# GpSimd decodes from the start, the shared port passed on by explicit dependencies, and a new order

## The chip, the cores and the metric

The kernel runs on one core of one Trainium2 chip. The metric is the time of one launch on the device in microseconds. The engines are named as the profile names them: PE (TensorE; PEld is its loading of weights), DVE (VectorE), ACT (ScalarE), POOL (GpSimd) and SP (SyncE, which only issues DMAs here).

## What is computed

Three stages follow each other: a recurrent attention (mLSTM), then two feed-forward layers on its output. The attention is computed in chunks of 64 time steps; the recurrence below is what every chunk must reproduce.

```python
for t in range(S):                                   # B=4, H=8, S=768, D=40
    m_new = np.maximum(f_gate[:, :, t] + m, i_gate[:, :, t])
    f_stab = np.exp(f_gate[:, :, t] + m - m_new)
    i_stab = np.exp(i_gate[:, :, t] - m_new)
    C = f_stab * C + i_stab * outer(vt, kt)
    n = f_stab * n + i_stab * kt
    y[:, :, t] = sigmoid(o_gate[:, :, t]) * (C @ qt) / np.maximum(np.abs(n @ qt), 1.0)
x = y.transpose(0, 2, 1, 3).reshape(B * S, H * D)    # 3072 x 320
h = x @ w_in;  x = np.maximum(0.01 * h, h) @ w_out   # layer 0, d_ff = 2048
h = x @ w_in2; out = (h * np.cos(h)) @ w_out2        # layer 1
```

The weights come as float64 and are turned into float32 on the chip.

## The kernel before

**Tiles and stages.** The 3072 tokens are 24 chunks of 128 rows. Layer 0 takes them in blocks of 4, 2, 3, 3, 3, 3, 3, 3 chunks (`BLOCKS1`), layer 1 in eight blocks of 3. A block has 16 *slots*, one for each 128 columns of `d_ff`. In a slot PE multiplies into the hidden tile (`m_in`, L806, written "in(k)" here), ACT makes the rounded activation `gh` and the full one in place (L814, L815), DVE takes their difference `gl` (`m_lo`, L854, "gl(k)"), and PE multiplies both with the output weights (`m_out`, L874, "mo(k)"). Every matmul is split this way into a rounded and a rest part.

**Weights.** Each of the 16 pieces of a layer's weights is loaded as 704 KB of 64-bit words (`w_load`, L422) and decoded by six steps: on DVE a shift (`w_bits`, L432), on ACT the tail and the sign (`w_tail`, L436; `w_sign`, L440), on DVE or POOL an addition (`w_round`, L444), on DVE the mask (`w_mask`, L448). Then ACT rounds (`w_hi`, L217) and DVE or POOL subtracts (`w_lo`, L463). A slot's in(k) waits for piece k. Layer 0's pieces are decoded while block 0 runs.

**Attention.** For chunk c, DVE scans the gates (L597), scales k (`kt`, L616) and v (`vext`, L609), PE makes the scores (L636, L627), DVE weighs them (L643), PE makes output and state (`a_out`, L664, L672). DVE adds the state's part (`ys`, L710), ACT and DVE make the denominator (`norm`, L718; `rec`, L720, L721), DVE scales and gates (`scale`, L728; `gate`, L733, which writes the tile `x`); `decay` (L690) prepares the next state. Then the chunk is transposed into `xt`: PE turns it (`x_turn`, L516, into the only tile `tr`), ACT rounds (L217), PE subtracts (`x_neg`, L534, L535, chunks 0 to 3) and ACT copies the rest. in(0) of block 0 waits for `xt` of the chunks 0 to 3. `g_turn` (L355 to L372, twice: turn(0) and turn(1)) spreads gate values; turn(1) uses the tile `tr` too.

**Order.** The class `Schedule` places every step on an engine by planned durations, priorities (`MUST`, `OFF`, `OFF0` and the other numbers at the head) and rings of buffers. The instructions are then issued in the order of the planned starts, and each engine works its own list in that order. Steps that the plan marks "port" (those of DVE with SBUF operands alone, and all of POOL) never overlap in the plan, as DVE and POOL share a port of SBUF.

**Fillers and pace.** 95 matmuls `busy` (`g_busy`, L267) that compute nothing stand on PE between the steps of the start and of block 0. A filler, and a DMA planned between 10 and 100 us, waits for the last DVE instruction that the plan has ended by then (`PACE`, `PACED`). All fillers write one tile of the ring "h", which has two tiles; the hidden tiles of block 0 come from the same ring. In the built program the hidden tiles of the slots 0 to 9 have one PSUM bank and `busy` has the other, and the two banks alternate from slot 10 on.

The function that a filler runs:

```python
i = hpi.bitcast(BF16)[:, 0:1]
nc.tensor.matmul(gt["busy"], i.to_broadcast([P, P]), i.to_broadcast([P, 512]), start=True, stop=True)
```

Of the kernel before, what the change touches and what calls it, by code (L numbers as in the profile page):

```python
# [34 lines left out]
NG = 3  # L35
# [9 lines left out]
WC = 3 * P + DM  # L45
# [12 lines left out]
ATT_GAP = 6.901
ATT_STEP = 1.34
OUT_LAG = 4.678  # L60
SLOT0 = 1.284
DEC_LEAD = 51.726
BUSY = [0.9, 44.0, 0.22, 58.0]
BY_PE = (0, 1, 2, 3)
MUST = {0: -89.386, 1: -35.775, 2: 41.006, 3: -118.66, 4: 7.351, 5: 41.735, 6: 41.268, 7: -49.472, 8: 9.383, 9: 11.955, 10: -120.864, 11: -1.76, 12: -54.393, 13: 8.105, 14: 10.291, 15: 40.118, 16: -25.59, 17: 6.765, 18: 45.788, 19: 75.325, 20: 7.383, 21: -25.675, 22: 55.394, 23: 9.929, 24: 7.4, 25: 9.087, 26: 31.973, 27: 23.522, 28: 9.759, 29: -29.728, 30: 24.391, 31: 42.171, 32: 38.02, 33: 21.052, 34: 23.884, 35: 39.051}
SPREAD = 4
PACE = 0.05
PACED = [10.0, 100.0]
TURNS = {0: -9.044, 1: -47.963}
GATES_TOO = -4.817  # L70
W2 = {0: -16.972, 1: -35.024}
OFF = {
    "fb": 152.276, "kvo": -84.501, "qk": 75.164, "vext": 37.96, "scan": -34.694, "kt": 81.751, "s": 9.354, "weigh": 65.471, "out": 135.411,
    "sig": 169.166, "ym": -23.852, "ys": -10.938, "norm": -12.629, "scale": -18.623, "gate": 76.438, "state": 108.617, "decay": 20.307, "tr": 29.765,
    "x2": 16.41, "l_a": -90.166, "l_g": -57.684, "l_cos": 34.983, "l_mul": -67.795, "l_gh": 122.022,
    "l_gl": -11.238, "w_round": 136.001, "w_mask": 74.621, "w_hi": 58.111, "w_lo": -46.707, "w_load": -50.808,
}

OFF0 = {
    "decay": 136.328, "fb": -55.476, "gate": 90.467, "kt": 88.848, "kvo": 55.846, "norm": 95.847, "out": 125.427, "qk": 40.375, "s": 87.542, "scale": -4.774, "scan": 70.824, "sig": 93.266, "state": -25.01, "tr": -2.926, "vext": 205.41, "weigh": 110.435, "ym": -19.56, "ys": 54.077,  # L80
}
# [5 lines left out]
class Schedule:  # L87
# [13 lines left out]
    def run(self):  # L101
# [3 lines left out]
        while todo:  # L105
# [68 lines left out]
            if not drop:  # L174
                order.append((start, len(order), eng, fn, args, end, pace))
        return sorted(order, key=lambda o: o[:2])
# [3 lines left out]
def mlstm_moe(ctx, tc, qk, kvo, gates, w1, w2, out):  # L180
# [42 lines left out]
    def dve(n, fast=False):  # L223
        return ("DVE", 0.065 + n * (0.00053 if fast else 0.00105), "port")
# [240 lines left out]
    def plan_decode(l, i, p, after=0.0):  # L465
        k = (l, i)
        wide = dma(2 * WC if double[l] else WC, pace=True)
        if not double[l]:
            sch.add(("wload", k), p - 6, SP, w_load, l, i, take=[("wf", k, 1)], after=after, **wide)
            return ("wload", k)  # L470
        sch.add(("wload", k), p - OFF["w_load"], SP, w_load, l, i, take=[("raw64", k, 1)], after=after,
                **wide)
        sch.add(("bits", k), p, ("DVE", 0.435, "port"), w_bits, l, i, deps=[("wload", k)], take=[("wf", k, 1)])
        sch.add(("tail", k), p, act(WC), w_tail, l, i, deps=[("wload", k)])
        sch.add(("sign", k), p + 0.1, act(WC), w_sign, l, i, deps=[("wload", k)], take=[("sg", k, 1)])
        sch.add(("round", k), p + OFF["w_round"], [dve(WC)] + pool(WC, l), w_round, l, i, deps=[("bits", k), ("tail", k), ("sign", k)],
                free=[("raw64", k)])
        sch.add(("mask", k), p + OFF["w_mask"], dve(WC), w_mask, l, i, deps=[("round", k), ("sign", k)], free=[("sg", k)])
        return ("mask", k)

    def plan_split(l, i, p, dep):
        k = (l, i)
        sch.add(("whi", k), p, act(WC), w_hi, l, i, deps=[dep], take=[("w", k, 1)])
        sch.add(("w", k), p + OFF["w_lo"], [dve(WC)] + pool(WC, l), w_lo, l, i, deps=[("whi", k)], free=[("wf", k)])

# [57 lines left out]
    def plan_x(l, n, c, j, p, dep, src, ring, m):  # L543
# [193 lines left out]
    def plan_attention(n, c, j, m):  # L737
# [32 lines left out]
        sch.add(("out", c), e - off["out"], ("PE", 0.65 + (0.29 if not last else 0)), a_out, c,  # L770
                deps=[("weigh", c), ("vext", c)] + kt,
# [126 lines left out]
    def plan_layer(l, n, c0, m):  # L898
        N = m * P
        blocks = (BLOCKS1, BLOCKS2)[l]  # L900
        for i in range(NF):
# [63 lines left out]
    c = 0  # L965
# [73 lines left out]
```

## Time and profile before

| | us |
|---|---|
| median of 3 runs | 817.56 (815.19 to 817.56) |
| the profiled execution | 817.87 |
| its span | 816.1 |
| PE busy | 803.5 |
| DVE busy | 611.3 |
| ACT busy | 443.0 |
| POOL busy | 27.1 |

The span is what the instructions cover; 1.77 us of the execution lie around it. A row of a timeline gives the start, the duration, the engine, the line, the operation and its tiles, how many instructions were merged, and in brackets the engine's idle time before it with what ended that. Back-to-back instructions of DVE overlap a little in such rows, so the distance from start to start is what one of them costs. [...]

### The profile page before, as it was taken

The numbers are of one execution on the slowest core, as the hardware profiler recorded it, in microseconds if no ns is written. First come the engines' busy times: TensorE is split into PE (matmuls) and PEld (weight loads), VectorE is DVE, ScalarE is ACT, GpSimd is POOL, SyncE is SP. The second block draws the span as 40 slices with busy tenths as digits, with TensorE's granted clock in tenths as the row PEclk, the third lists the DMA queues.
The fourth block names the chain that finished last, engine by engine and source line by source line (L and its number), as shares of the span: only waits on it lengthen the run. The fifth ranks groups of instructions, "written<-read, shape, count | busy, mean of one in ns | idle before, by whom it ended". The sixth has DMA issues, their size and how long they took to land.

```text
span 816.1 us, 19170 instructions
## 1 busy us (share of the span) xinstructions
PE 803.5 (98%) x7803; PEld 767.3 (94%) x7815; DVE 611.3 (75%) x1287; ACT 443.0 (54%) x976; POOL 27.1 (3%) x29
## 2 busy tenths in 40 slices
PE   9899999999999999999999999999999999999998
PEld 5668899998999999999999999999999999999998
DVE  7979987747647478473738798889798988888886
ACT  3578844435534345344344665656565656565664
POOL 1000010000302000100000000000000000000000
PEclk9999999999999999999999999999999999999999
DMA  6655564516615254343324300000000000010000
GB/s 187 196 185 204 168 180 155 183 43 168 196 60 151 90 169 156 101 138 118 105 77 146 111 9 29 21 17 25 25 26 25 25 22 29 10 41 9 13 13 25
DMA packets 29944, 74.49 MB, mean 91 GB/s; under 512 B 4384, under 2 KB 13728, under 8 KB 29856
## 3 DMA queue, kind: packets, MB, share of 16 engines
q1 hardware_dynamic: 29856, 73.27, 28.9%
q8 instruction: 61, 1.00, 0.5%
q14 instruction: 27, 0.22, 0.1%
HBM read 59.54 MB, written 13.71 MB: 90 GB/s over the span
## 4 chain that ended last, share of the span: by engine, by line
PE 93%; DVE 5%; issue 1%; ACT 1%; DVEq 0%; ACTq 0%
PE acc L874 40%; PE ph L806 36%; PE pair L806 6%; PE busy L267 2%; PE tr L516 2%; PE pair L627 2%; PE pair L664 2%; PE pair L636 1%; PE pair L672 1%; DVE gl L854 1%; DVE wf L444 1%; DVE wf L448 1%; DVE w L463 1%; DVE wf L432 0%; DVE fb L643 0%
## 5 line engine op out<-in xcount | busy, mean ns | idle before, releaser
L874 PE MATMUL acc<-w,gh 128*128 128x320 f32 x1568 | 347.9, 309 | 0.0
L806 PE MATMUL ph<-xt,w 128*128 128x384 f32 (+2 forms) x1760 | 344.8, 338 | 2.4 <-DVE gl L854 2.3
L806 PEld LDWEIGHTS ph<-xt,w 128*128 128x128 f32 x1760 | 296.8, 188 | 9.2 <-DVE gl L854 3.4
L874 PEld LDWEIGHTS acc<-w,gh 128*128 128x128 f32 x1568 | 264.6, 188 | 2.2
L874 PE MATMUL acc<-w,gl 128*128 128x320 f32 (+1 forms) x784 | 238.6, 308 | 0.1
L874 PEld LDWEIGHTS acc<-w,gl 128*128 128x128 f32 x784 | 145.9, 188 | 0.4 <-DVE gl L854 0.4
L814 ACT ACTIVATE gh<-ph 128x384 fp32r<-128x384 f32 (+2 forms) x124 | 60.9, 491 | 152.0 <-PE ph L806 112.1
L854 DVE TENSOR_TENSOR gl<-ph,gh 128x384 fp32r<-128x384 f32 (+2 forms) x124 | 68.7, 554 | 98.4 <-ACT ph L815 98.0
L836 ACT ACTIVATE r<-r,hpi 128x384 f32<-128x384 f32 x128 | 78.9, 616 | 69.1 <-DVE r L832 69.0
L217 ACT CAST gh<-g 128x384 fp32r<-128x384 f32 x128 | 65.5, 512 | 38.9 <-PE acc L874 19.2
L854 DVE TENSOR_TENSOR gl<-g,gh 128x384 fp32r<-128x384 f32 x127 | 69.5, 552 | 9.1 <-ACT gh L217 9.1
L842 DVE TENSOR_TENSOR g<-ph,r 128x384 f32<-128x384 f32 x96 | 53.3, 555 | 13.2 <-ACT r L836 12.1
L815 ACT ACTIVATE ph<-ph 128x384 f32<-128x384 f32 (+2 forms) x124 | 60.3, 486 | 0.0
L806 PE MATMUL pair<-xt,w 128*128 128x384 f32 x288 | 55.9, 336 | 0.0
L831 DVE SCALAR_TENSOR_TENSOR r<-t,ph 128x384 f32<-128x384 f32 x96 | 53.2, 554 | 3.3
L822 ACT ACTIVATE t<-ph 128x384 f32<-128x384 f32 x96 | 46.8, 488 | 14.2 <-PE ph L806 8.5
L828 DVE TENSOR_SCALAR t<-t 128x384 f32<-128x384 f32 x128 | 45.7, 357 | 7.3 <-ACT t L822 4.1
L832 DVE TENSOR_SCALAR r<-r 128x384 f32<-128x384 f32 x128 | 46.8, 365 | 4.4
L806 PEld LDWEIGHTS pair<-xt,w 128*128 128x128 f32 x288 | 49.4, 188 | 0.0
L217 ACT CAST xt<-tr 128x256 fp32r<-128x256 f32 x104 | 27.6, 315 | 20.6 <-PE tr L516 18.1
L463 DVE TENSOR_TENSOR w<-wf,w 128x704 fp32r<-128x704 f32 x32 | 28.4, 889 | 4.4 <-ACT w L217 3.9
L448 DVE SCALAR_TENSOR_TENSOR wf<-wf,sg 128x704 f32<-128x704 f32 x32 | 28.1, 882 | 0.3
(113 smaller groups left out, 637.2 us busy)
## 6 DMA issues: line engine op xcount, KB each, us to landing
raw<-w SPq DMA_DIRECT2D x32, 704.0 KB, 4.5
kvo<-kvo SPq DMA_DIRECT2D x24, 484.0 KB, 4.0
raw<-qk SPq DMA_DIRECT2D x48, 192.0 KB, 3.8
w2d<-wf SPq DMA_DIRECT2D x16, 352.0 KB, 2.6
wf<-w2d SPq DMA_DIRECT2D x16, 352.0 KB, 2.9
fb<-sfd SPq DMA_DIRECT2D x40, 128.0 KB, 3.5
x2d<-o SPq DMA_DIRECT2D x24, 160.0 KB, 1.8
x<-x2d SPq DMA_DIRECT2D x24, 160.0 KB, 2.2
```

Source lines behind the costliest of these rows:

```text
L217: nc.scalar.copy(dst, src)
L806: nc.tensor.matmul(ph[:, :N], w[:, a:a + P], x[:, b, :N], start=k == 0, stop=k == 7)
L814: nc.scalar.activation(t["gh"][:, :N], h, AF.Prelu, alpha=0.01)
L815: nc.scalar.activation(h, h, AF.Prelu, alpha=0.01)
L822: nc.scalar.activation(t["a"][:, :N], t["h"][:, :N], AF.Copy, scale=1.0 / TWO_PI, bias=0.25)
L828: nc.vector.tensor_scalar(a, a, MAGIC, -MAGIC, ALU.add, ALU.add)
L831: nc.vector.scalar_tensor_tensor(r, a, -TWO_PI, t["h"][:, :N], ALU.mult, ALU.add)
L832: nc.vector.tensor_scalar(r, r, -4.712388, 1.5707959, ALU.max, ALU.min)
L836: nc.scalar.activation(r, r, AF.Sin, bias=hpi)
L842: nc.vector.tensor_tensor(t["g"][:, :N], t["h"][:, :N], t["r"][:, :N], ALU.mult)
L854: on[eng].tensor_tensor(t["gl"][:, :N], t["g"][:, :N], t["gh"][:, :N].bitcast(F32), ALU.subtract)
L874: nc.tensor.matmul(po, a[:, s], w[:, b, e], start=i == 0 and k == 0 and j < 3, stop=i == NF - 1 and k == 2, skip_group_check=True,)
```

## The change

The planner may now put `w_round`, `w_lo` of layer 0 and `kt`, `vext`, `scale`, `decay` of the first chunks on POOL (`late` is always true). `rec` counts as a port step. Where a port step follows one of the other engine, it gets an explicit dependency on that one, while the planned start is under 100 us. Some planned durations are a little longer. All numbers that set the order are new.

```diff
-MUST = {0: -89.386, 1: -35.775, 2: 41.006, ...
+MUST = {0: -140.461, 1: -24.673, 2: 80.866, ...
...
-                order.append((start, len(order), eng, fn, args, end, pace))
+                order.append((start, len(order), eng, fn, args, end, pace, bool(port)))
...
-        sch.add(("tail", k), p, act(WC), w_tail, l, i, deps=[("wload", k)])
-        sch.add(("sign", k), p + 0.1, act(WC), w_sign, l, i, deps=[("wload", k)], take=[("sg", k, 1)])
-        sch.add(("round", k), p + OFF["w_round"], [dve(WC)] + pool(WC, l), w_round, l, i, deps=[("bits", k), ("tail", k), ("sign", k)],
+        sch.add(("tail", k), p, ("ACT", 0.75), w_tail, l, i, deps=[("wload", k)])
+        sch.add(("sign", k), p + 0.1, ("ACT", 0.735), w_sign, l, i, deps=[("wload", k)], take=[("sg", k, 1)])
+        sch.add(("round", k), p + OFF["w_round"], [dve(WC)] + pool(WC), w_round, l, i, deps=[("bits", k), ("tail", k), ("sign", k)],
...
-        sch.add(("w", k), p + OFF["w_lo"], [dve(WC)] + pool(WC, l), w_lo, l, i, deps=[("whi", k)], free=[("wf", k)])
+        sch.add(("w", k), p + OFF["w_lo"], [dve(WC)] + pool(WC), w_lo, l, i, deps=[("whi", k)], free=[("wf", k)])
...
-        g, late = s // NG, n > 1
+        g, late = s // NG, True
...
-        sch.add(("rec", c), e - off["norm"], ("DVE", 0.32), a_norm, c, deps=[("norm", c)])
+        sch.add(("rec", c), e - off["norm"], ("DVE", 0.32, "port"), a_norm, c, deps=[("norm", c)])
...
-        block, dve = tc.nc.cur_bb.bb.instructions, []
-        for start, _, eng, fn, args, end, pace in sch.run():
+        block, dve, held = tc.nc.cur_bb.bb.instructions, [], None
+        for start, _, eng, fn, args, end, pace, port in sch.run():
             n = len(block)
             fn(eng, *args)
+            after = []
+            if port:
+                if held and held[0] != eng and start < PACED[1]:
+                    after.append(held[1])
+                held = eng, block[-1].name
             if eng == "DVE":
                 dve.append((end, block[-1].name))
             if pace and (eng == "PE" or PACED[0] < start < PACED[1]):
-                before = [d for d in dve if d[0] <= start - PACE]
-                if before:
-                    tc.add_manual_dep(block[n], max(before)[1], SYNC, reason="pace")
+                after += [max(d for d in dve if d[0] <= start - PACE)[1]] if dve and dve[0][0] <= start - PACE else []
+            for name in after:
+                tc.add_manual_dep(block[n], name, SYNC, reason="pace")
```

Both programs hold the same matmuls and 95 fillers; 90 stood before in(0) and 89 do now. In the built program the slots 0 to 10, one more, share the bank beside `busy`. ACT loads a table 5 times before and 7 times now; both new loads stand before block 0 is over.

POOL's list, first the steps after `eye` in the kernel before: a decay, a vext and two roundings of layer 1's weights, with a kt behind them.

```order
L690 TENSOR_TENSOR tmp<-state_141,col 104x328
L609 TENSOR_TENSOR kvo<-kvo,col 128x328
L444 TENSOR_TENSOR wf<-wf,raw_1313 128x704
L444 TENSOR_TENSOR wf<-wf,raw_1955 128x704
L616 TENSOR_TENSOR kvo<-kvo,fb 128x320
```

The same place now. All nine stand before the end of the start: kt(1), decay(2), kt(2), scale(1), decay(3), round of piece 0, decay(4), round of piece 1, decay(5).

```order
L616 TENSOR_TENSOR kvo<-kvo,fb 128x320
L690 TENSOR_TENSOR tmp<-state_141,col 104x328
L616 TENSOR_TENSOR kvo<-kvo,fb 128x320
L728 TENSOR_TENSOR kvo<-kvo,d 128x320
L690 TENSOR_TENSOR tmp<-state_142,col 104x328
L444 TENSOR_TENSOR wf<-wf,raw_391 128x704
L690 TENSOR_TENSOR tmp<-state_141,col 104x328
L444 TENSOR_TENSOR wf<-wf,raw_575 128x704
L690 TENSOR_TENSOR tmp<-state_142,col 104x328
```

The number of layer 0's pieces rounded on POOL went from none to two.

PE's list around the turning of chunk 2 (L516), before: it stands behind turn(1) (L369, L372) and out(3) (L664, L672).

```order
L372 MATMUL pt<-pick,of 64x3x2x4 x2
L664 MATMUL acc<-kvo,fb 64x41 x16
L672 MATMUL pair<-kvo 40x41 x16
L267 LDWEIGHTS hpi
L267 MATMUL busy<-hpi 128x512
L267 LDWEIGHTS hpi
L267 MATMUL busy<-hpi 128x512
L516 MATMUL tr<-ident,x 128x128 x2
L516 MATMUL tr<-ident,x 64x128
```

And now:

```order
L516 MATMUL tr<-ident,x 128x128 x2
L516 MATMUL tr<-ident,x 64x128
L267 LDWEIGHTS hpi
L267 MATMUL busy<-hpi 128x512
L267 LDWEIGHTS hpi
L267 MATMUL busy<-hpi 128x512
L664 MATMUL acc<-kvo,fb 64x41 x16
L672 MATMUL pair<-kvo 40x41 x16
L534 MATMUL tr<-xt,minus 128x256
L535 MATMUL tr<-xt,minus 64x128
```

The turning of chunk 2 moved ahead of out(3); turn(1) follows behind this, after eight fillers.

DVE's list from gl(0) to gl(2), before: two steps of decoding between gl(0) and gl(1), five between gl(1) and gl(2).

```order
L854 TENSOR_TENSOR gl<-ph,gh 128x512
L444 ISA wf<-raw_802,wf 128x1408
L463 TENSOR_TENSOR w<-wf,w 128x704
L854 TENSOR_TENSOR gl<-ph,gh 128x512
L432 TENSOR_SCALAR wf<-raw_853 128x704
L448 SCALAR_TENSOR_TENSOR wf<-wf,sg 128x704
L444 ISA wf<-raw_853,wf 128x1408
L463 TENSOR_TENSOR w<-wf,w 128x704
L432 TENSOR_SCALAR wf<-raw_878 128x704
L854 TENSOR_TENSOR gl<-ph,gh 128x512
```

And now:

```order
L854 TENSOR_TENSOR gl<-ph,gh 128x512
L432 TENSOR_SCALAR wf<-raw_825 128x704
L854 TENSOR_TENSOR gl<-ph,gh 128x512
L444 ISA wf<-raw_825,wf 128x1408
L463 TENSOR_TENSOR w<-wf,w 128x704
L432 TENSOR_SCALAR wf<-raw_864 128x704
L448 SCALAR_TENSOR_TENSOR wf<-wf,sg 128x704
L444 ISA wf<-raw_864,wf 128x1408
L448 SCALAR_TENSOR_TENSOR wf<-wf,sg 128x704
L463 TENSOR_TENSOR w<-wf,w 128x704
L854 TENSOR_TENSOR gl<-ph,gh 128x512
```

One short step is left between gl(0) and gl(1), and seven stand between gl(1) and gl(2).

## Rows read from the trace of the kernel before

**Rows 1.** The page's first part: busy time, share of the span, instructions.

```profile
PE 803.5 (98%) x7803; PEld 767.3 (94%) x7815; DVE 611.3 (75%) x1287; ACT 443.0 (54%) x976; POOL 27.1 (3%) x29
```

**Rows 2.** Windows: length, then busy time of PE, PEld, DVE, ACT, POOL.

```profile
51.90:118.20 66.30, 65.00 (x615) 57.93 (x618) 59.20 (x94) 49.35 (x88) 3.33 (x3) 1.00 0.60 191
118.20:812.40 694.20, 691.81 (x6399) 680.64 (x6399) 510.34 (x1093) 366.67 (x827) 21.26 (x17) 1.00 0.24 74
```

**Rows 3.** PE's timeline: state of chunk 3, turns of chunks 2 and 3, five slots.

```profile
37.83 0.56 PE L672 MATMUL pair<-kvo 64*40 64x41 f32 x18 [1.34 <-issue]
...
39.16 0.85 PE L516 MATMUL tr<-ident,x 128*128 128x128 f32 x3
...
43.29 0.49 PE L516 MATMUL tr<-ident,x 128*128 128x128 f32 x3
...
45.83 2.18 PE L806 MATMUL ph<-xt,w 128*128 128x512 f32 x8
...
49.91 2.11 PE L806 MATMUL ph<-xt,w 128*128 128x512 f32 x8 [1.45 <-DVE gl L854]
...
57.99 2.12 PE L806 MATMUL ph<-xt,w 128*128 128x512 f32 x8
...
83.22 2.11 PE L806 MATMUL ph<-xt,w 128*128 128x512 f32 x8 [0.36 <-DVE gl L854]
```

**Rows 4.** PE's timeline: twelve fillers in a row.

```profile
12.85 2.82 PE L267 MATMUL busy<-hpi 128*128 128x512 bf16 x12 [0.16 <-issue]
```

**Rows 5.** DVE: busy time to the end of gate(3); state(3), gate(3), a scan, gl(1).

```profile
0.00:39.72 39.72, 33.09 (x91) 0.97 0.68 190
...
38.76 0.49 DVE L682 TENSOR_TENSOR state<-pair,tmp 104x328 f32<-104x328 f32 x1
39.17 0.55 DVE L733 TENSOR_TENSOR x<-acc,kvo 128x160 f32<-128x160 f32 x2
...
40.84 1.22 DVE L597 TENSOR_TENSOR_SCAN fb<-fb,eye 128x512 f32<-128x512 f32 x1
...
53.18 0.69 DVE L854 TENSOR_TENSOR gl<-ph,gh 128x512 fp32r<-128x512 f32 x1 [1.71 <-ACT ph L815]
```

**Rows 6.** DVE's timeline: lo, mask, round, gl, bits back to back.

```profile
63.52 0.88 DVE L463 TENSOR_TENSOR w<-wf,w 128x704 fp32r<-128x704 f32 x1
64.33 0.88 DVE L448 SCALAR_TENSOR_TENSOR wf<-wf,sg 128x704 f32<-128x704 f32 x1
65.13 0.88 DVE L444 CUSTOM_DVE_ANT_0 wf<-raw,wf 128x1408 uint16<-128x1408 uint16 x1
65.93 0.68 DVE L854 TENSOR_TENSOR gl<-ph,gh 128x512 fp32r<-128x512 f32 x1
66.53 0.52 DVE L432 TENSOR_SCALAR wf<-raw 128x704 int32<-128x704 int32 x1
```

**Rows 7.** Timelines of POOL and of DVE where both work.

```profile
101.20 0.91 POOL L690 TENSOR_TENSOR tmp<-state,col 104x328 f32<-104x328 f32 x1 [97.95 <-DVE state L682]
...
111.27 1.81 DVE L690 TENSOR_TENSOR tmp<-state,col 104x328 f32<-104x328 f32 x1
...
111.00 1.73 POOL L444 TENSOR_TENSOR wf<-wf,raw 128x704 int32<-128x704 int32 x1
...
186.80 0.74 POOL L616 TENSOR_TENSOR kvo<-kvo,fb 128x320 f32<-128x320 f32 x1 [45.77 <-DMA kvo<-kvo]
...
203.61 1.20 POOL L728 TENSOR_TENSOR kvo<-kvo,d 128x320 f32<-128x320 f32 x1 [2.19 <-DVE d L721]
```

**Rows 8.** ACT's timeline: a table load and what follows; the second half of gh(1).

```profile
4.99 1.28 ACT L694 ACT_TABLE_LOAD   x1
6.29 0.83 ACT L694 ACTIVATE kvo<-kvo 128x320 f32<-128x320 f32 x2
...
52.55 0.59 ACT L815 ACTIVATE ph<-ph 128x512 f32<-128x512 f32 x1
```

**Rows 9.** A window of PE: busy time, granted clock, DMA share, GB/s.

```profile
38.00:39.00 1.00, 0.67 (x19) 0.50 0.91 260
```

More of the change, by code (lines that the diff above doesn't have):

```diff
@@ L53 @@
 SLOW = 7.0
-T_START = 7.517
-ATT_LEAD = 4.426
+T_START = 10.924
+ATT_LEAD = 3.613
 BACKLOG = 0.9
 HORIZON = 260.0
[L58 to L62, printed above, removed]
+ATT_GAP = 7.723
+ATT_STEP = 0.909
+OUT_LAG = 5.923
+SLOT0 = 1.365
+DEC_LEAD = 51.635
 BUSY = [0.9, 44.0, 0.22, 58.0]
 BY_PE = (0, 1, 2, 3)
-MUST = {0: -89.386, 1: -35.775, 2: 41.006, 3: -118.66, 4: 7.351, 5: 41.735, 6: 41.268, 7: -49.472, 8: 9.383, 9: 11.955, 10: -120.864, 11: -1.76, 12: -54.393, 13: 8.105, 14: 10.291, 15: 40.118, 16: -25.59, 17: 6.765, 18: 45.788, 19: 75.325, 20: 7.383, 21: -25.675, 22: 55.394, 23: 9.929, 24: 7.4, 25: 9.087, 26: 31.973, 27: 23.522, 28: 9.759, 29: -29.728, 30: 24.391, 31: 42.171, 32: 38.02, 33: 21.052, 34: 23.884, 35: 39.051}
+MUST = {0: -140.461, 1: -24.673, 2: 80.866, 3: -143.603, 4: 22.96, 5: 35.048, 6: 3.448, 7: -55.853, 8: 10.472, 9: 17.063, 10: -34.267, 11: 10.187, 12: -79.261, 13: 13.013, 14: -22.114, 15: 42.33, 16: -1.013, 17: 8.187, 18: 45.801, 19: 60.353, 20: 7.92, 21: -26.721, 22: 74.934, 23: 7.459, 24: 8.352, 25: 9.027, 26: 38.802, 27: -23.085, 28: 6.308, 29: -9.698, 30: 24.905, 31: 22.79, 32: 52.71, 33: 31.771, 34: 8.97, 35: 39.836}
 SPREAD = 4
@@ L68 @@
 PACED = [10.0, 100.0]
-TURNS = {0: -9.044, 1: -47.963}
-GATES_TOO = -4.817
-W2 = {0: -16.972, 1: -35.024}
+TURNS = {0: -26.217, 1: -69.589}
+GATES_TOO = -7.087
+W2 = {0: 11.591, 1: -52.769}
 OFF = {
[L73 to L76, printed above, removed]
+    "fb": 159.592, "kvo": -80.174, "qk": 77.305, "vext": 111.828, "scan": 39.803, "kt": 20.747, "s": 13.949, "weigh": 65.544, "out": 124.262,
+    "sig": 174.679, "ym": -11.123, "ys": -28.413, "norm": 21.702, "scale": -19.752, "gate": 80.961, "state": 88.035, "decay": 30.34, "tr": 78.774,
+    "x2": 16.41, "l_a": -92.773, "l_g": -58.657, "l_cos": -74.175, "l_mul": -40.12, "l_gh": 4.038,
+    "l_gl": -3.008, "w_round": 136.632, "w_mask": 73.564, "w_hi": 35.639, "w_lo": -66.602, "w_load": -44.168,
 }
 OFF0 = {
-    "decay": 136.328, "fb": -55.476, "gate": 90.467, "kt": 88.848, "kvo": 55.846, "norm": 95.847, "out": 125.427, "qk": 40.375, "s": 87.542, "scale": -4.774, "scan": 70.824, "sig": 93.266, "state": -25.01, "tr": -2.926, "vext": 205.41, "weigh": 110.435, "ym": -19.56, "ys": 54.077,
+    "decay": -51.438, "fb": 99.777, "gate": 70.587, "kt": 99.022, "kvo": 40.629, "norm": 127.277, "out": -38.358, "qk": 40.777, "s": 145.714, "scale": 33.021, "scan": 58.322, "sig": 96.331, "state": -38.169, "tr": 6.831, "vext": 187.061, "weigh": 104.11, "ym": -26.246, "ys": 82.034,
 }
@@ L548, in plan_x @@
             sch.add(("xn", c), p + 0.7, ("PE", 0.48), x_neg, l, n, c, j, deps=[("xhi", l, c), "minus"])
-            sch.add(("x", l, c), p + 0.8, ("ACT", 0.62), x_rest, l, n, c, j, deps=[("xn", c)], free=[("tr", (l, c))])
+            sch.add(("x", l, c), p + 0.8, ("ACT", 0.66), x_rest, l, n, c, j, deps=[("xn", c)], free=[("tr", (l, c))])
             return
@@ L762, in plan_attention @@
             sch.add(("kt", c), e - off["kt"], [dve(DM), heads] + pool(DM, late), a_kt, c, deps=[("kvo", c), ("scan", c)])
-        sch.add(("s", c), e - off["s"], ("PE", 0.66 + (0.45 if s else 0)), a_scores, c,
+        sch.add(("s", c), e - off["s"], ("PE", 0.72 + (0.45 if s else 0)), a_scores, c,
                 deps=[("qk", c, 0), ("qk", c, 1), ("scan", c), "clear"] + kt + ([("state", c - 2)] if s else []),
@@ L769, in plan_attention @@
         sch.add(("sig", c), e - off["sig"], ("ACT", 0.36), a_sig, c, deps=[("kvo", c), ("exp", 0, 0), ("exp", 0, 1)], table="sig")
-        sch.add(("out", c), e - off["out"], ("PE", 0.65 + (0.29 if not last else 0)), a_out, c,
+        sch.add(("out", c), e - off["out"], ("PE", 0.72 + (0.29 if not last else 0)), a_out, c,
                 deps=[("weigh", c), ("vext", c)] + kt,
@@ L913, in plan_layer @@
             if l == 0:
-                sch.add(("gh", k), p + OFF["l_a"], ("ACT", 2 * act(N, True)[1]), m_leak, n, m, i, deps=after("gh", "in"), take=[("gh", k, 1)])
+                sch.add(("gh", k), p + OFF["l_a"], ("ACT", 0.04 + 2 * act(N, True)[1]), m_leak, n, m, i, deps=after("gh", "in"), take=[("gh", k, 1)])
                 sch.add(("gl", k), p + OFF["l_g"], dvp(N), m_lo, l, n, m, i, deps=after("gl", "gh"), take=[("gl", k, 1)], free=hs)
```

## The prediction

> **What bounds the kernel now.** I began with the page's busy times. PE works 803.5 of 816.1 us [rows 1], so the time is PE's work plus what PE waits or fills. Windows over PE's stages then tell where that is. From the end of block 0 to the last matmul PE is busy 691.8 of 694.2 us [rows 2]: nothing can be won there, since both programs hold the same matmuls. From mo(0) to the end of block 0 it is busy 65.0 of 66.3 [rows 2]. What is left is the start, the 45.83 us before in(0) and the 4.08 from there to in(1) [rows 3]. The change can only win by bringing in(0) and in(1) forward and then keeping that lead through block 0.
>
> PE's and DVE's timelines show what holds these two points. Before in(0) it is chunk 3: gate(3) ends at 39.72 on DVE [rows 5], but PE turns the chunk only at 43.29 [rows 3], because chunk 2, whose turn shares the one tile `tr`, was turned at 39.16, behind turn(1), out(3) and a stall of 1.34 us that the profile puts down to issue [rows 3]. Before in(1) it is gl(0): the row of in(1) names it [rows 3]. The slots 1 to 9 have one PSUM tile among them, so each in(k) starts right behind gl(k-1): in, then `gh` and the full activation on ACT, then gl, then the next in. Over the slots 1 to 9 that makes (83.22 - 49.91) / 8 = 4.16 us a slot [rows 3].
>
> **The change: DVE up to gate(3).** Two roundings, one bits, two kt, three decays and one ym leave DVE's list ahead of gate(3); a scan and a copy of a state come in. From start to start a rounding costs 0.80 and a bits 0.44 [rows 6], a small step 0.41 (state(3) to gate(3)), a scan 1.22 [rows 5]. So 2 x 0.80 + 0.44 + 6 x 0.41 - 1.22 - 0.41 = 2.9 us less, of the 33.1 that DVE works up to there [rows 5].
>
> POOL does this slower: a kt 0.74, a decay 0.91, a scale 1.20, a rounding 1.73 [rows 7]. And while POOL holds the port, a DVE step on SBUF alone stands still: a decay that costs 0.41 took 1.81, to the end of POOL's rounding [rows 7]. The new dependencies make the same wait explicit. What they cost is what DVE lacks in steps that need no port meanwhile:
> - kt(1), decay(2) and kt(2) run beside scans, weighings and a gate (1.22, about 0.6 and 0.55 [rows 5, 6]; a weighing taken as a gl): nothing.
> - scale(1), then decay(3): 1.20 against a weighing and a ym, about 1.0, then 0.91 against gate(1), 0.55 [rows 5, 7]. Together 0.6.
> - round(0) and decay(4), 2.64 in all, against ys(2), state(2) and a scan, about 2.1 [rows 5, 7]: 0.6 with the handing over.
> - round(1), 1.73, against state(3) and ys(3), about 0.9 [rows 5, 7], for rec(3), which is a port step now: 0.9, and 0.2 for the handing over.
>
> The sum is 2.3. The ends are 0 (all of it finds cover) and 8.9 (two kt, three decays, a scale and two roundings, nothing covered); I take the walk. Besides, col(1), which now stands right ahead of gate(3), needs turn(1), and turn(1) stands behind eight fillers, 8 x 0.235 = 1.9 us [rows 4], that wait for DVE up to state(3): 0.4 more. gate(3) then ends at 39.72 - 2.9 + 2.3 + 0.4 = 39.5. DVE is relieved, and gate(3) comes no sooner to speak of.
>
> **The change: from gate(3) to in(0).** Here lies the gain. Chunk 2 is turned ahead of out(3) and turn(1), so `tr` is long free when gate(3) ends. Two paced fillers follow gate(3), 0.5 us [rows 4], and tr(3) starts at 40.1 in place of 43.29. From there on nine fillers and the same steps stand as before, 45.83 - 43.29 = 2.5 us [rows 3]: in(0) at 42.6, a lead of 3.2. The last of these fillers waits for mask(2), four steps behind gate(3), 3 x 0.80 + 0.44 = 2.8 [rows 6], so 42.3: no later.
>
> **From in(0) to in(3): the gain goes.** gl(0) stands nine steps behind gate(3) on DVE, seven of 0.80 and two bits [rows 6]: 39.5 + 6.5 = 46.0. Over PE and ACT it is ready at 42.6 + 2.18 + 2 x 0.55 = 45.9 [rows 3, 8]. With a few tenths for round(3), which waits for a sign that ACT makes late, gl(0) ends at 47.1 and in(1) starts at 47.3: a lead of 2.6.
>
> Before, two steps lie between gl(0) and gl(1), and DVE idled 1.71 us ahead of gl(1) [rows 5]. Now only a bits does, as if in(1) followed in(0) at once. It does not, because of the one tile: gl(1) is ready 2.11 + 1.1 + 0.1 = 3.3 us behind the start of in(1) [rows 3, 8], at 50.6, and DVE idles some 3 us. Behind gl(1) stand seven steps of decoding, 6 x 0.80 + 0.44 = 5.2, and then gl(2): it starts at 50.6 + 0.6 + 5.2 = 56.4 and ends at 57.1 [rows 6]. in(3) starts at 57.2 in place of 57.99 [rows 3]. The lead is 0.8.
>
> **The rest.** From in(3) on DVE needs 3 to 3.7 us a slot against the chain's 4.16, so the chain sets the pace as before. Two fillers more stand in these slots and one more behind them, up to 3 x 0.235 = 0.7 where PE is late, nothing where gl is: I take 0.3. The slot 10 also shares the one tile: 0 to 0.4, I take 0.3. After block 0 nothing changes, give or take one stall of the kind of 1.34 [rows 3]. Sum: -0.8 + 0.3 + 0.3 = -0.2, from 817.87 (span 816.1 and 1.77 around it) to 817.7. The profiled execution is 0.3 above the median of the runs shown, 817.56, so that is no change; a measurement of this kernel tells about 0.3%, 2.5 us, from none.
>
> **ACT's new table loads** are weighed apart. A load takes 1.28 us, and the next step starts 0.02 behind its end [rows 8]. Two loads now stand ahead of norm(2), which rec(2) on DVE waits for; by my walk norm(2) is done some 0.2 us before DVE comes to rec(2), so they cost nothing, with no margin. [...]
>
> **Rivals.**
> - *The lead is kept.* POOL's steps find cover, so that the 2.3 and the 0.4 fall away. All from gate(3) to gl(2) hangs on DVE's list, so it moves as a whole: a lead of 0.8 + 2.7 at in(3), less 0.6, gives 815.0. For it: only the four waits above were found without cover, each under a microsecond. Against: the steps that cover them wait for PE themselves.
> - *Slower: the clock falls before in(1).* PE has one filler between in(0), which ends at 44.8, and in(1) at 47.3, a gap of 2.3 us. [...] Behind the gap of 1.45 before in(1), however, that matmul group took 2.11 us, as the others do at full clock [rows 3]. If the clock falls, in(1) takes 4.2 in place of 2.1, and half of mo(0) another 1: with the chain behind it, +2.7, 820.4. It decides from a gap between 1.45 and 2.3.
> - *Slower: ACT comes late to norm(2).* sig(3) stands between the two loads and norm(2) and waits for the load of chunk 3, which is now issued behind state(1). If it lands 2 us late, rec(2) and all behind it do: 819.7.
> - *It does not do what it says.* The port is handed on by the hardware anyway [rows 7], and the new order runs like the old one: 817.9.
>
> **How the numbers follow.** The forecast, 815.9 to 819.5 by the open terms (waits on POOL 1.5 lower or higher, a stall), has 0.48; the kept lead 0.25, the clock 0.13, ACT 0.09, no effect 0.05. Faster by over 0.3% means under 815.1: most of the kept lead and a little of the forecast, 0.22. Slower by over 0.3% means over 820.0: most of the clock, half of ACT, a little of the forecast, 0.18. Within: 0.60. The range runs from 814.3, the kept lead and some, to 820.7, the clock's price.
>
> **What the profile after would show.** Right: POOL works about 10 us before in(0); tr(2) stands ahead of out(3); in(0) near 42.6 and in(1) near 47.3, named as waiting for gl(0); an idle time of about 3 us before gl(1) on DVE; in(3) at 57 to 58; from in(3) on the same distances as before; the granted clock 1.00 through 44 to 50. Wrong: gate(3) well before 38 (POOL's waits covered) or after 41, an in(2) that does not wait for gl(1), an ACT that waits for kvo before sig(3), or a stretch of PE at 0.50 behind in(0).

## The result and the profile after

The changed kernel takes 826.24 us (median of 4 executions, 824.98 to 828.17), the kernel before 817.56 beside it (4 executions, 815.19 to 818.54): ratio 1.012, interval 1.0096 to 1.0145. It is slower by 8.7 us between the medians and by 9.8 by the ratio, outside the range of the prediction.

The page of the changed kernel: the span, and the busy time that answers to [rows 1].

```profile
span 826.4 us, 19281 instructions
PE 807.3 (98%) x7815; PEld 770.3 (93%) x7815; DVE 607.8 (74%) x1276; ACT 457.4 (55%) x1041; POOL 28.9 (3%) x33
```

PE's timeline of the changed kernel in block 0, with the same slots as [rows 3]: in(0), in(1), in(3), in(9), and the first matmuls of block 1.

```profile
42.96 2.20 PE L806 MATMUL ph<-xt,w 128*128 128x512 f32 x8
47.45 2.76 PE L806 MATMUL ph<-xt,w 128*128 128x512 f32 x8 [2.06 <-DVE gl L854]
...
58.67 2.07 PE L806 MATMUL ph<-xt,w 128*128 128x512 f32 x8 [1.53 <-DVE gl L854]
...
83.31 2.11 PE L806 MATMUL ph<-xt,w 128*128 128x512 f32 x8
...
118.34 1.14 PE L806 MATMUL ph<-xt,w 128*128 128x256 f32 x8
```

Up to here the two profiled executions are level: block 1 starts at 118.34, and at 118.20 before [rows 2]. So the whole loss against this execution of the kernel before lies behind block 0, where the forecast had nothing. (That execution turns out to be a late one; see before_shift42.) The same timeline from there on, every idle time of PE over 0.15 us between 118 and 420 us:

```profile
123.13 0.68 PE L664 MATMUL pair<-kvo,fb 64*64 64x41 f32 x32 [0.47 <-DVE fb L643]
132.49 0.68 PE L664 MATMUL pair<-kvo,fb 64*64 64x41 f32 x32 [0.21 <-DVE y L705]
136.34 0.99 PE L806 MATMUL ph<-xt,w 128*128 128x256 f32 x7 [2.56 <-issue]
188.88 0.68 PE L664 MATMUL pair<-kvo,fb 64*64 64x41 f32 x32 [0.92 <-ACT y L703]
253.21 0.30 PE L874 MATMUL acc<-w,gh 128*128 128x320 f32 x1 [2.05 <-issue]
296.57 0.68 PE L664 MATMUL pair<-kvo,fb 64*64 64x41 f32 x32 [0.99 <-ACT y L703]
311.77 0.52 PE L516 MATMUL tr<-ident,x 128*128 128x128 f32 x3 [0.47 <-DVE x L733]
349.64 0.68 PE L664 MATMUL pair<-kvo,fb 64*64 64x41 f32 x32 [0.92 <-ACT y L703]
365.23 0.52 PE L516 MATMUL tr<-ident,x 128*128 128x128 f32 x3 [0.85 <-DVE x L733]
```

They add up to 9.44 us. The kernel before has five in this stretch, which add up to 2.22; its largest is this one, again put down to issue:

```profile
200.65 0.27 PE L672 MATMUL pair<-kvo 64*40 64x41 f32 x3 [1.37 <-issue]
```

Windows of the changed kernel (length, busy time of PE, PEld, DVE, ACT, POOL, then the granted clock of TensorE as a share of full speed, the share of the DMA engines and GB/s) show what comes on top:

```profile
43.00:53.00 10.00, 7.94 (x34) 6.15 (x33) 6.15 (x10) 6.66 (x11) 0.00 (x0) 0.83 0.57 188
130.00:140.00 10.00, 7.23 (x156) 6.73 (x156) 6.24 (x13) 2.91 (x6) 0.00 (x0) 0.87 0.65 145
250.00:260.00 10.00, 7.95 (x98) 7.79 (x95) 5.20 (x13) 3.65 (x8) 0.00 (x0) 0.83 0.32 99
```

Behind each of the two longest idle times, and behind the wait before in(1), PE ran for a while at a lower clock: the granted clock is 0.50 in the windows 49 to 52, 138 to 140 and 254 to 256. So the difference of the spans, 826.4 - 816.1 = 10.3, is 0.1 up to block 1, 7.2 of idle time (9.44 - 2.22), and 3.0 left over for the two falls of the clock behind block 0.

Two suspects stand in these rows. **Theory F**: an instruction packet of PE comes late ("issue": PE waited for nothing that the profile shows). **Theory Y**: the product `y` on ACT.

For F, the trace records 61 packets of 16,384 bytes on an instruction queue of their own. That they are PE's instructions is my estimate, from their number: PE's 7815 weight loads and 7815 matmuls, 15,630 over 61 packets, make 256 to a packet. The packet that ended the first stall started at 133.84, 515 instructions behind the one before; the one of the second at 250.86, 490 behind. All others between 118 and 420 us lie 23 to 417 apart. PE works again 1.3 to 1.4 us after such a packet has landed (134.96 and 136.34, 251.93 and 253.21). The DMA queues of the changed kernel (packets, MB, share of the 16 engines) from 125 to 133.8 us and from 133.8 to 135:

```profile
q1 hardware_dynamic: 699, 1.99, 85.0%
...
q1 hardware_dynamic: 66, 0.13, 34.3%
q8 instruction: 1, 0.02, 5.8%
```

In the first stretch, in which a packet fell due by count, a weight load of 704 KB, a `kvo` load of 484 KB and five smaller transfers were issued, and no packet came. Ahead of the second, from 242 us on, it was again these two and five smaller ones. It came as the loads ran out.

For Y, the line of `y` on ACT, before and after (count, shortest, median and longest, first and last start):

```profile
L703 ACT ACTIVATE y<-pair,col x24: 287/305/338, 96.3 to 197.0; 128x41 f32<-128x41 f32 x24
...
L703 ACT ACTIVATE y<-pair,col x96: 287/313/340, 33.9 to 357.7; 128x41 f32<-128x41 f32 x96
```

That is three chunks before and twelve after, eight activations a chunk. Around the wait at 188.88, DVE and ACT did this:

```profile
186.51 0.69 DVE L643 TENSOR_TENSOR fb<-pair,fb 128x512 f32<-128x512 f32 x1 [1.42 <-PE pair L636]
...
187.24 1.59 ACT L703 ACTIVATE y<-pair,col 128x41 f32<-128x41 f32 x8 [0.92 <-DVE fb L643]
```

The weighing on DVE and `y` on ACT both only read `pair`, but one follows the other: 0.69 and then 1.59. The row of ACT names the weighing as what ended its wait, and out of the chunk (L664) waits for both. The plan lets them run side by side. In the two traces they never do: of the 15 chunks with `y` on ACT (three before, twelve after), the second of the two starts 0.03 to 0.09 us behind the end of the first in 14, four times `y` (0.04 here) and ten times the weighing, and 2.39 behind in the other. That reading the one tile is the reason is my reading; no run tests it.

### The profile page after: what moved, and what is told of

Read it like the earlier page. It is cut to its first block, busy times and chain, and to the rows that moved or that the text cites. A ratio compares the mean times of both kernels' runs of the same rounds, so it can differ in the third digit from the quotient of the medians.

```text
span 826.4 us, 19281 instructions
## 1 busy us (share of the span) xinstructions
PE 807.3 (98%) x7815; PEld 770.3 (93%) x7815; DVE 607.8 (74%) x1276; ACT 457.4 (55%) x1041; POOL 28.9 (3%) x33
## 4 chain that ended last, share of the span: by engine, by line
PE 87%; DVE 4%; ACT 2%; DMA 1%; issue 1%; SPq 0%; DVEq 0%; ACTq 0%
PE acc L874 39%; PE ph L806 36%; PE pair L806 6%; PE tr L516 2%; PE pair L627 1%; PE pair L664 1%; ACT y L703 1%; PE pair L636 1%; DMA raw<-w 1%; PE pair L672 1%; PE busy L267 1%; DMA fb<-sfd 1%; DVE fb L643 1%; DVE wf L448 1%; DVE gl L854 1%
## 5 line engine op out<-in xcount | busy, mean ns | idle before, releaser
L217 ACT CAST gh<-g 128x384 fp32r<-128x384 f32 x128 | 65.5, 511 | 39.5 <-PE acc L874 20.2
```

The lines of the kernel that those rows point to most:

```text
L217: nc.scalar.copy(dst, src)
```

## The experiments

Medians of each kernel, the ratio to the kernel before on the same chip, and where block 1 starts in the profiled execution:

| kernel | median us | ratio (interval) | block 1 |
|---|---|---|---|
| changed | 826.24 | 1.0120 (1.0096 to 1.0145) | 118.34 |
| shift70 | 820.28 | 1.0048 (1.0018 to 1.0078) | 117.67 |
| shift196 | 821.59 | 1.0080 (1.0053 to 1.0106) | 117.67 |
| ym_dve | 821.30 | 1.0068 (1.0043 to 1.0093) | 118.31 |
| shift70_ym | 815.02 | 0.9993 (0.9979 to 1.0006) | 116.64 |
| no_pool | 817.95 | 1.0015 (0.9997 to 1.0033) | 119.86 |
| flood | 817.37 | 1.0012 (0.9991 to 1.0034) | 117.48 |
| before_shift42 | 814.06 | 0.9961 (0.9943 to 0.9980) | 114.05 |
| after_tile | 818.43 | 1.0022 (1.0000 to 1.0044) | 110.52 |
| tile | 808.11 | 0.9889 (0.9856 to 0.9921) | 110.63 |
| tile_no_pool | 810.21 | 0.9932 (0.9911 to 0.9954) | 112.21 |
| tile_no_deps | 810.01 | 0.9933 (0.9907 to 0.9958) | 112.47 |
| before_s42_tile | 810.50 | 0.9941 (0.9917 to 0.9964) | 110.06 |

The kernel before has a median of 815.4 to 815.9 beside the experiments, and single executions from 813.6 to 820.7. Each kernel was profiled in one execution, so the column of block 1 and all timelines below are of one execution each. Where an edit adds lines, the line numbers of a kernel lie a few higher.

**Late packets: shift70 and shift196.** The fillers get a counter; five of them (shift196: fourteen, 66 to 79) are split.

```diff
+        gt["count"] = gt.get("count", -1) + 1
+        if 71 <= gt["count"] < 76:
+            for k in range(8):
+                nc.tensor.matmul(gt["busy"][:32, 64 * k:64 * k + 64], i.to_broadcast([P, 32]), i.to_broadcast([P, 64]), start=True, stop=True)
+            return
         nc.tensor.matmul(gt["busy"], i.to_broadcast([P, P]), i.to_broadcast([P, 512]), start=True, stop=True)
```

> The changed kernel, and five of the fillers that TensorE runs while it waits between 34 and 41 us are each written as eight matmuls of 64 columns instead of one of 512: the same columns, but 35 more matmuls and 35 more weight loads, 70 instructions more in TensorE's stream ahead of block 0. Nothing else moves. Theory F (late instruction fetch): the stalls of 2.56 us at 133.8 and 2.05 us at 251.2 arise because a packet of 256 TensorE instructions (16,384 bytes on the instruction queue) was due just when four bulk loads were in flight and started 5.7 and 5.3 us late, where it starts about 1 us late when no data moves. 70 instructions further on the packets are due at other moments: no idle time of TensorE longer than 0.5 us without a releaser after 118 us, the granted clock 1.00 in the stretches 130 to 140 and 250 to 260 (0.87 and 0.83 in the changed kernel), total 818 to 821. Rival P (the stall belongs to the instruction or the place): both stalls stay at the same matmuls, total 826. Rival R (chance of the one execution): stalls of this kind anywhere, total 823 to 828.

> As the run with 70 more instructions, with fourteen fillers split: 98 matmuls and 98 weight loads, 196 instructions more. Theory F: the stalls at 133.8 and 251.2 go here too, but the packet that was due at about 306 now is due at about 302, when a weight load of 704 KB and two others are in flight (issued at 302.1, landing at 308.3): a stall of 0.5 to 2 us between 305 and 309 is likely, with no stall there in the run with 70; total 818 to 823. Rival P: the stalls at 133.8 and 251.2 stay, 826.

shift70 took 820.28, as F said. Behind 84 us no idle time over 0.15 is put down to issue, and the clock stands at 1.00 in the same windows:

```profile
130.00:140.00 10.00, 9.79 (x173) 9.11 (x167) 7.93 (x18) 4.53 (x13) 0.00 (x0) 1.00 0.70 142
250.00:260.00 10.00, 10.00 (x66) 9.99 (x65) 7.75 (x16) 4.47 (x13) 0.74 (x1) 1.00 0.47 158
```

Beside its shorter idle time (5.19 us in place of 9.44 behind 118 us), shift70 gives back the same 3.0 that I put down to the two falls of the clock.

In shift196 both stalls are gone too. The new stall that I expected between 305 and 309 did not come: the packet there started in time. And a packet at 247.43 lies 489 instructions behind the one before, as the late ones of the changed kernel do, yet PE does not stall. So the place in the stream matters, as F has it, but my count is too coarse to say which packet stalls PE. What the stalls share is another number: in all nine idle times of 1.17 us and more behind 34 us that are put down to issue (two each in the changed kernel, the kernel before, ym_dve and after_tile, one in before_s42_tile), PE works again 1.2 to 1.5 us after a packet has landed.

**`y` back on DVE: ym_dve, and both edits: shift70_ym.**

```diff
+            if fn is a_inter and args[0] >= BLOCKS1[0]:
+                eng = "DVE"
             fn(eng, *args)
```

> The changed kernel with its order kept, except that from block 1 on the product y (state part of the scores times its decay), which the plan gives ScalarE as eight activations (1.59 us together, nine chunks from block 1 on), runs on VectorE as one instruction (0.49 us), at the same place in time. Theory Y: the waits of 0.92, 0.99 and 0.92 us for ACT y before the matmuls of L664 at 187.9, 295.6 and 348.7 come from the long ScalarE form, and go; TensorE's idle time after 118 us falls by 2.5 to 3, total 823 to 824.5 if the two fetch stalls stay. Rival: y is late whatever engine does it, because scores, weighing and y follow each other there; the waits stay, with VectorE as the releaser, and the total is 826.

> Both edits: 70 more filler instructions and y on VectorE from block 1 on. If F and Y both hold and add up: 815.5 to 818.5, no worse than the kernel before (817.6). If only F holds 818 to 821, if only Y holds 823 to 824.5, if neither 826. More than 821 although each alone gains would mean that the changed timing of the one brings a late fetch back.

ym_dve took 821.30, some 2 us better than I had put it for Y. All waits for `y` on ACT are gone (2.83 us), and of those for `x` and the weighing, 0.47, 0.85 and 0.47, there are left 0.49, 0.30 and 0.21. The two stalls for issue stayed at the same two places, somewhat shorter (3.31 us in place of 4.61), and this time without a fall of the clock there:

```profile
135.04 0.95 PE L806 MATMUL ph<-xt,w 128*128 128x256 f32 x6 [1.41 <-issue]
249.38 0.31 PE L874 MATMUL acc<-w,gl 128*128 128x320 f32 x1 [1.90 <-issue]
```

With both edits 815.02. The ratio falls by 0.0072 for the one, 0.0052 for the other and 0.0127 for both: the two gains add up within the noise of these medians (ym_dve has shortened the two stalls as well, by 1.3 us), and together the two causes are the whole loss against the kernel before as it stands.

**More data in flight: flood.** To shift70_ym, behind each load of second-layer weights:

```diff
+            if l:
+                nc.sync.dma_start(spare[i], w[i].bitcast(I32))
```

> The kernel with 70 more filler instructions and y on VectorE, and behind each of the 16 loads of second-layer weights (704 KB each, 125 to 400 us) one more copy of the same 704 KB from DRAM to DRAM on the same queue, which nothing waits for. Theory F: TensorE's instruction packets then queue behind more data, several start over 4 us late, and idle time of TensorE put down to no releaser comes back after 118 us: 3 us or more in several places, total above 819. Other waits for late data may add to it. Rival (fetches have nothing to do with data in flight, only their place in the stream matters): no such idle time after 118 us; only waits for DMA grow.

This missed. The data queue rose from 41.1% of the 16 engines to 50.6% between 118 and 420 us, but nothing over 0.15 is put down to issue there. The medians lie 2.4 us apart, the two profiled spans 4.0. Of these, 0.84 are in block 0, where the clock seems to have fallen again (in(1) took 2.58 in place of 2.11), and 2.1 are waits for `x` and gl behind it; the rest stays open. So more traffic alone did not stall PE. My reading is that a packet must also fall due just before a run of small matmuls, which use up the stream fast, as in both stalls of the changed kernel (64 of them and their weight loads took 0.92 us from 132.49 on, the eight of in(0) 2.20); no run tests that. That the late packets are caused by data in flight rests on the rows of the stalls alone: the shifts show that the place in the stream matters, and this run went against it.

**The kernel before, shifted: before_shift42.** As shift70, with the fillers 59 to 61.

> The kernel before, with three of its fillers between 32 and 42 us split into eight matmuls each: 21 matmuls and 21 weight loads, 42 instructions more. Theory F: the stall of 1.37 us within the matmuls of L672 at 199.3, where the instruction packet started 4.0 us late with loads in flight, goes or moves; total 0.5 to 1.5 below the kernel before on the same chip. Rival P: it stays, and the total is that of the kernel before.

The stall at 199.3 shrank to 0.63 and the total is 0.4% lower. What I had not expected is the start: in(0) at 41.68 and block 1 at 114.05, 4.15 earlier than in the profile of before. The stall of 1.34 us inside the matmuls of L672, with the clock of 0.50 behind it [rows 3, 9], ended like the others: a packet landed at 36.57, and PE worked again at 37.83. It is not all of the 4.15: at out(3) (L664), ahead of the stall, the two profiles are already 1.28 apart (35.66 and 34.38). Most of that stands behind PE's first fillers, before and in before_shift42:

```profile
1.04 5.71 PE L267 MATMUL busy<-hpi 128*128 128x512 bf16 x13 [1.04 <-DVE gm L291]
...
1.03 4.46 PE L272 MATMUL busy<-hpi 128*128 128x512 bf16 x13 [1.03 <-DVE gm L296]
```

These 13 take from 4.46 to 5.77 us in the fourteen profiled executions, whatever the edit, where 12 later ones take 2.82 [rows 4]. That leaves 2.9 us for the stall and its clock, and two starts compared across profiles can differ by over 1 us for no reason of the edit.

**The single tile: tile.** shift70_ym without the late fillers.

```diff
+            if fn is g_busy and start > 44.0:
+                continue
```

> The kernel with 70 more filler instructions and y on VectorE, without the last fillers (those planned later than 44 us, which run singly between the matmul groups of block 0 from 49 to 88 us). They keep one of the two PSUM tiles of the ring h, so in(1) of block 0 has to take the tile of in(0) and waits 2.09 us for gl(0). Theory T: with the tile free, in(1) starts at about 44.8 instead of 47.1 with no wait for gl, gl(1) comes some 2 us earlier, VectorE's idle time of 2.89 us before it shrinks below 1 us, and the decode steps behind it follow earlier: in(3) at 55 to 56 instead of 57.3, block 1 at 114.5 to 115.6 instead of 116.6, total 813 to 814 against 815.0. Rival D (the decode of the weights is late anyway): in(1) early, in(3) still at 57, total 815. Rival C: without those fillers the granted clock falls once more in block 0, 816.5.

808.11, faster than both kernels. PE's timeline of this kernel, the same slots:

```profile
42.95 2.21 PE L811 MATMUL ph<-xt,w 128*128 128x512 f32 x8
45.46 2.12 PE L811 MATMUL ph<-xt,w 128*128 128x512 f32 x8
...
53.20 2.05 PE L811 MATMUL ph<-xt,w 128*128 128x512 f32 x8
...
76.48 2.05 PE L811 MATMUL ph<-xt,w 128*128 128x512 f32 x8
...
110.63 1.14 PE L811 MATMUL ph<-xt,w 128*128 128x256 f32 x8
```

in(1) no longer waits, DVE's idle time before gl(1) is 0.90 instead of 2.89, in(3) stands 4.1 earlier than in shift70_ym, and a slot takes 3.84 where it took 4.0 to 4.4. I had expected 2 us of the 6: I counted the wait before in(1) and not the hold-up in every slot.

**The tile in the other kernels: after_tile and before_s42_tile.** The same edit on the changed kernel alone, and on before_shift42 (there, fillers behind in(1) in the order are dropped).

> The changed kernel, and of the edits only that the fillers planned later than 44 us are left out, so that in(1) of block 0 has a PSUM tile of its own. Nothing else: y stays on ScalarE, the instruction stream is 10 instructions shorter. Theory T: block 1 starts at 111 to 112.5 instead of 118.3, the total is 5.5 to 7 lower than the 826.2 of the changed kernel: 819 to 821, and the late fetches and the waits for y behind block 0 stay as they are. Rival: the gain of the tile shows only once those are gone; 824 or more.

> The kernel before with 42 more filler instructions, without the three fillers that stand behind in(1) of block 0 in its plan. Theory T: the single tile cost the kernel before the same; in(1) starts without the wait of 1.45 us, the step from in(k) to in(k+1) is 3.84 us as in the changed kernel without late fillers, instead of 4.0 to 4.4, and the total falls by 3 to 6 from 814.1: 808 to 811. Then the tile, and not the early work on GpSimd, makes the difference. Rival: in the kernel before the decode on VectorE is late for that, total 813 to 814.

Block 1 starts 7.8 and 4.0 earlier. after_tile keeps its waits for `y` and its late packets (1.61 and 1.17 for issue); before_s42_tile has one of 1.85. So the tile cost the kernel before 3.6 us (814.06 to 810.50), shift70_ym 6.9 and the changed kernel 7.8 (by the medians; between the two profiles of the changed kernel and after_tile late packets and falls of the clock differ as well). The change did not bring the tile, but its order pays more for it. With the tile shared, in(0) to block 1 takes 72.37 in before_shift42 and 74.08 in shift70_ym, where in(1) waits 2.09 and in(3) 2.06 in place of 1.45 and nothing; with the tile free it takes 68.13 in before_s42_tile and 67.68 in tile.

**The parts of the change: no_pool, tile_no_pool, tile_no_deps.** GpSimd's early steps back on DVE; or the explicit dependencies left out.

```diff
+            if eng == "POOL" and start < 45.0 and fn in (w_round, a_kt, a_scale, a_decay):
+                eng = "DVE"
             fn(eng, *args)
             after = []
             if port:
-                if held and held[0] != eng and start < PACED[1]:
-                    after.append(held[1])
```

> The kernel with 70 more filler instructions and y on VectorE, with the order kept, but every decode and attention step that the change put on GpSimd before 45 us (two roundings of 1.70 us, and the products kt, scale and decay of some 0.73 us) runs on VectorE at the same place in the order (0.88 and some 0.48 us). This undoes the headline of the change alone: VectorE gets about 5 us more work before 45 us. By the recorded prediction the early GpSimd work brings in(0) about 3 us earlier and block 0 gives that back: in(0) at 45 to 46 instead of 42.6, in(3) 57.5 to 59, block 1 at most 1.5 us later than 116.6, total 815 to 816.5. Rival (the lead is kept): all of it is lost, block 1 3 us later, total 818. Rival (GpSimd's use of the shared port slowed VectorE as much as it relieved it): no difference, 815.

> The kernel with 70 more filler instructions, y on VectorE and no late fillers, with the early GpSimd steps put back on VectorE, order kept. Together with the pair that had the late fillers (817.95 with the steps on VectorE, 815.02 with them on GpSimd) it tells what the headline of the change is worth when in(1) need not wait. Lead kept: in(0) some 2 us later and block 1 as much, total 810 to 811. Given back: VectorE catches up in block 0, block 1 within 0.7 us, total 808 to 808.8. Decode late on VectorE without its pauses: more than 2 us, total above 811.

> The kernel with 70 more filler instructions, y on VectorE and no late fillers, without the explicit dependencies by which the change passes the shared port between VectorE and GpSimd before 100 us; order and engines kept. If they matter: VectorE and GpSimd run into one another in the start and their steps take longer (the rounding on GpSimd over 1.9 us, VectorE's beside it over 1.0 us where it takes 0.9), in(0) 0.5 us or more later, total 808.7 or more. If they only write down an order that holds anyway: 807.5 to 808.5, durations as before. A gain would mean that they cost waits: GpSimd starts earlier, in(0) before 42.9.

With the steps on DVE in(0) comes 2.0 us later, and 1.6 later where the tile is free; block 1 comes 3.2 and 1.6 later (in no_pool in(1) took 3.42 us, as at a lower clock, in shift70_ym 2.11). Counted from out(0), which stands behind the first fillers (13.59 and 13.66 us, 13.97 and 13.36), in(0) comes 2.0 and 2.2 later. So GpSimd's early work is worth about 2 us in this order (the medians differ by 2.9 and 2.1), and block 0 does not give them back, though I had expected it to.

Without the dependencies in(0) comes 1.9 later. Counted from out(0) (13.97 and 14.53) it is 1.3 of the 2.2; the medians, 810.01 against 810.21 with no GpSimd steps and 808.11 with both, leave nothing of the gain. So most of it, if not all, is gone. GpSimd's rounding and a step of DVE, first with the dependencies (tile), then without:

```profile
34.43 1.69 POOL L449 TENSOR_TENSOR wf<-wf,raw 128x704 int32<-128x704 int32 x1 [6.26 <-DVE wf L453]
15.76 0.45 DVE L614 TENSOR_TENSOR kvo<-kvo,col 128x328 f32<-128x328 f32 x1
...
34.26 3.49 POOL L449 TENSOR_TENSOR wf<-wf,raw 128x704 int32<-128x704 int32 x1 [4.82 <-ACT raw L441]
16.32 0.94 DVE L614 TENSOR_TENSOR kvo<-kvo,col 128x328 f32<-128x328 f32 x1
```

Where the two met, without the dependencies, the rounding took 3.49 in place of 1.69 and the product 0.94 in place of 0.45. What these runs show of a shared port is such times. In the kernel before, beside POOL's roundings of 1.73 at 111.00 and 250.57, a decay of DVE, with SBUF operands alone, took 1.81 [rows 7] and 1.43 (the median of its line is 0.49), while steps of DVE with a PSUM operand kept their time beside such roundings: `y` 0.49 at 210.49, `gate` 0.49 at 216.34, `ys` 0.51 at 250.81. In this order the early GpSimd work pays only with the explicit dependencies, or little without them.

## Why the prediction was wrong

**The step that failed is "After block 0 nothing changes, give or take one stall of the kind of 1.34."** I argued from 691.8 busy of 694.2 us [rows 2] that nothing could be won there, and took it that nothing could be lost. The new order put `y` of nine chunks behind block 0 on ACT, where there were two (waits of 2.83 us for it, and 0.8 to 1.3 more for `x` and the weighing, which went with it), and two instruction packets came late (4.61 us instead of 1.37, and two falls of the clock, 3.0). The first could be asked before the run: the engine of every `y` stands in the order of the instructions. Of the second only the kind could be known, from the stall inside a merged group of matmuls in [rows 3], which I counted as chance; where the packets would fall I could not have said, as shift196 shows.

**The baseline.** I measured the lead of in(0), 45.83 - 42.6 = 3.2, against an execution whose start was 4 us late, 2.9 of them by the packet. Against before_shift42 the changed kernel's in(0) is not earlier but 1.3 later (42.96 and 41.68). The reason that I gave for the lead fails with it. I took the 3.6 us from the end of gate(3) to the turn of chunk 3 (39.72 and 43.29) for the cost of the one tile `tr` behind turn(1) and out(3). In before_shift42, with the same order, they are 0.7 (38.44 and 39.15):

```profile
37.89 0.55 DVE L738 TENSOR_TENSOR x<-acc,kvo 128x160 f32<-128x160 f32 x2
...
39.15 0.49 PE L521 MATMUL tr<-ident,x 128*128 128x128 f32 x3
```

In the changed kernel they are 0.8 (39.62 and 40.42), so the new place of the turn wins nothing there. That block 1 then stood level with the profile of before was luck: the gain that I saw "going" in block 0 had never been there, and the range was laid around that same late execution. How many executions of before carry the stall is not known. But of the 53 timed beside the experiments, 17 have a mean granted clock of 0.995 to 0.998, as the profiled one has (0.998), and took 816.6 to 820.7 us; the other 36, at 0.999 and 1.00, took 813.6 to 816.3. All ten of before_shift42 stand at 0.999 and 1.00.

**The walk of the new order up to block 1 came out as told.** gate(3) ended at 39.62 (forecast 39.5), in(0) at 42.96 (42.6), in(1) at 47.45 (47.3) with the wait for gl(0), DVE idled 3.53 us before gl(1) (about 3), and block 1 stands 0.1 from where it was (forecast 0.2 earlier). in(3) came at 58.67, not 57.2, as the clock fell behind in(0) (0.83 over 43 to 53 us): in(1) took 2.76 instead of 2.11.

**The clock rival** was half right. It gave 2.7 us, with 4.2 for in(1), which is 2.11 at the 0.50 of [rows 9]; no run shows in(1) at 0.50 to its end, it took 2.58 to 3.42 us where it was slow. From in(0) to block 1 the changed kernel takes 75.38, ym_dve, where the clock fell behind in(3)'s wait, 75.49, shift70 74.50 and shift70_ym 74.08 without a fall: 0.9 to 1.4 us. And the length of the gap does not decide, as I had it: shift70, shift70_ym and shift196 waited 2.08, 2.09 and 2.05 before in(1) and kept 1.00, the changed kernel waited 2.06 and fell to 0.50. In the kernel before 0.50 stood behind the stall of 1.34 [rows 3, 9], which is shorter than the 1.45 that I took as the lower end.

**The other rivals.** ACT did not come late to norm(2). "It does not do what it says" has its answer in tile_no_deps: without the dependencies in(0) comes 1.9 us later, and the median is 810.01 in place of 808.11. The lead against the profiled execution was not kept. The single tile that I named does hold block 0 up, as the runs without the late fillers show; I saw 4.16 us a slot and took it as given, where the fillers that hold the other tile could be left out.

**The sum, corrected.** 826.2 is the kernel before plus 6 us for late packets and their clock and 4 to 5 for `y`. With both repaired the change is worth nothing that can be told (0.9993), and beside before_shift42 (0.9961), where the packets of the kernel before are moved too, it is some 0.3% slower. With the tile freed as well, block 1 starts at 110.63, and at 110.06 in the kernel before with the same repair; the 2.4 us between these two medians (808.11 and 810.50) are about what before_s42_tile still idles more behind 118 us (3.13 and 0.52), 1.85 of it for a late packet.

## What to carry to other kernels

When an order is searched anew, look behind the stage that the change is about: count for every step with a choice of engines how often it changed sides, and ask whether two engines that read one PSUM tile were planned side by side (`y` on ACT and the weighing ran one after the other in all 15 chunks here). For an idle time inside a run of TensorE's matmuls that no engine explains, see whether an instruction packet landed just before its end, as in all nine such cases here; shift the stream by some dozen instructions, and measure no lead against an execution that has one. And a matmul that only fills time still holds its PSUM tile (leaving the late fillers out took 6.9 us off shift70_ym); see what else could use it.

## What the runs showed of the hardware that I had not expected

- Nine idle times of PE of 1.17 to 2.56 us, put down to issue, ended 1.2 to 1.5 us behind the landing of an instruction packet. The 35 small matmuls and 35 weight loads that moved the packets put in(0) at most 0.2 us later, and took 6 us off the changed kernel (826.24 to 820.28).
- The clock may or may not fall behind a gap of the same length: before in(1) PE waited 2.04, 2.06 and 2.10 us in no_pool, the changed kernel and flood, and in(1) took 3.42, 2.76 and 2.58; it waited 2.08, 2.08 and 2.09 in shift70, ym_dve and shift70_ym, and in(1) took 2.13, 2.11 and 2.11. Before in(3) it waited 2.06 us in ym_dve, and in(3) took 3.51; it waited 2.05 and 2.06 in shift70 and shift70_ym, and in(3) took 2.10 and 2.08. The granted clock over 40 to 90 us is 0.97 in the changed kernel and ym_dve and 1.00 in shift70, shift70_ym and shift196, which waited 2.05 and 2.06. In no_pool and flood the lengths alone speak for a fall.
- DVE and POOL on the shared port: a rounding of 1.69 us on POOL (tile) took 3.49 without the dependencies (tile_no_deps), and a product of 0.45 on DVE took 0.94.
- PE's first 13 fillers took 4.46 to 5.77 us from one profiled execution to the next, and out(3) stood 1.28 us apart where they differed by 1.25 (before and before_shift42).
